# A long convolution by a two-factor Fourier transform, followed by a soft mixture of experts: the transform's length as 111 x 197 instead of 127 x 181

## The chip, the cores and the metric

One NeuronCore of a Trainium2 chip runs the whole program in one launch. Its engines are named as in the profile: PE is the matrix engine (PEld its loading of the stationary operand), DVE the vector engine, ACT the scalar engine, POOL the general engine, SP the engine whose queue issues nearly all DMAs here. The metric is the device time of one execution in microseconds (us).

## The reference

Everything is fp32. `x` and `v` are (4, 11456, 128); the filter is made by a small network from `pos_emb` (11456, 64). The convolution is causal and as long as the sequence, and its result goes through a mixture of 8 experts with 32 slots.

```python
B, S, D = x.shape
h_mlp = np.maximum(pos_emb @ w1, 0.0) @ w2
h_filt = h_mlp * np.exp(-0.01 * np.arange(S))[:, None]
u = x * v
y = irfft(rfft(u, n=2 * S, axis=1) * rfft(h_filt, n=2 * S, axis=0), n=2 * S, axis=1)[:, :S]
x = (x * y).reshape(B * S, D)
logits = x @ phi                                  # 45824 tokens x 32 slots
d = softmax(logits, over tokens); slot_input = d.T @ x
slot_out[e] = relu(slot_input[e] @ w1[e]) @ w2[e]  # 8 experts, 1024 hidden
out = softmax(logits, over slots) @ slot_out
```

## The kernel before

The transform has length L = N1 * N2 = 127 * 181, just over 2 * 11456. A position is written as 127 * j + r, with residues r from -63 to 63. Because both factors are odd and the data are real, only J = 91 = (181 + 1) / 2 frequencies of the long factor are kept and only R = 64 residues, each with its mirror image, so that one row of 2R = 128 holds r and -r. The 128 channels are worked on in G = 8 groups of 16; with 4 batches a group has C = 64 columns.

For a group there are four steps, each of which is a family of small fp32 matmuls. An fp32 matmul leaves two records in the trace, each with its own weight load, so that a count of 2048 records is 1024 matmuls.

- **p1** (function `first`, line 121): the sums and differences of x * v (tile `sd`, line 216; the product itself is made by POOL, line 213) are the stationary operand, JP = 96 rows of tokens by 128 residues; the cosine and sine table `tab1x` of 2J = 182 columns moves. 64 matmuls a group. ACT copies each result into `T` in three instructions for two channels (lines 125, 126 and 130), of 364, 182 and 182 elements a partition.
- **p2** (line 231): for each of the 91 frequencies one matmul, with the 127-column table `W[:, k, :]` stationary and 128 columns of `T` moving. DVE multiplies the result by the filter's spectrum `Hs` (line 236, two instructions for four frequencies), POOL combines the products and writes them back to `T` (lines 242 and 243).
- **p3** (line 249): 128 matmuls a group, 91 columns of `T` stationary, 2R = 128 columns of `tab3` moving; ACT copies one half (`ec`, line 253), DVE adds and subtracts into `E` (line 255).
- **p4** (line 279): two matmuls for each residue, 91 columns of `tab4` stationary, 128 columns of `E` moving, over JP = 96 rows of `E`, of which the last five are zeros that a DMA from `in_zero` put there once (line 342). DVE multiplies by `x` (line 285), and `p4_out` stores two blocks of 90 rows to the DRAM scratch `scr` (lines 293 and 297), plus one row left over in some cases (line 307). Residues go in blocks `rb` of eight, so there are eight of these.

The loop at line 313 shifts the steps by one group: its pass g first runs p1 of group g mixed with p3 of group g - 1 (16 units, each 8 matmuls of p3 and 4 of p1; called **stage A** below), then p4 of group g - 1 mixed with p2 of group g (**stage B**; the count `upto` at line 353 spreads the 23 blocks of p2 over the first 14 of 16 half blocks of p4). In pass 0 p1 runs alone, and p2 of group 0 is mixed with the making of the filter's spectra, which go to DRAM as `hs` (line 167) and come back as `Hs` in each stage A (line 320). Before that the filter itself goes through its network (`hid_step`, 16 steps of four residues), the first transform (`first` with `tab1h`, 32 calls) and the second (`filter_second`). In the last pass p3 and p4 of group 7 run alone while the experts' weights load. The mixture of experts follows in 24 blocks of at most 15 * 128 tokens.

What a reader needs of the order: engines take their instructions in order, and so does the SP queue; a framework orders what is not held by `inorder` by its own estimate of durations. The pool `ld` has five buffers for all tiles of x, v and xi, `st` has three for `sd` and `xo`, and the PSUM pools `psa` (p1, p2) and `psb` (p3, p4) four each. A load waits at the head of the SP queue until its buffer is free, and what is behind it waits too.

## Time and profile before

| | us |
|---|---|
| median of 3 runs (1159.65 to 1163.18) | 1161.48 |
| the profiled execution, its own time | 1160.11 |
| its span, first to last instruction | 1158.3 |
| PE busy (share of the span) | 1085.9 (94%) |
| PE weight loads busy | 1022.3 (88%) |
| DVE busy | 922.8 (80%) |
| ACT busy | 590.4 (51%) |
| POOL busy | 578.3 (50%) |
| mean granted PE clock, share of full | 0.962 |

The table is one average over stages that are limited by different things. The profile can be cut into stages by the line of the matmuls that run: the filter to 127 us, pass 0's p2 to 179, then seven pairs of stages A and B of some 50 us each to 892, the lone p3 and p4 of group 7 to 955, and the mixture of experts to the end. A busy PE is not a PE at its peak, since matmuls are pipelined and the duration of one record (0.25 to 0.33 us) is more than the distance between two; what one costs is read from the distance between starts.

### The profile page before, as it was taken

To read this page: it belongs to the slowest core of one execution; us is meant where nothing else is said; L and a number is where in the kernel's file an instruction comes from. 1 tells how busy PE (TensorE), PEld (TensorE's weight loads), DVE (VectorE), ACT (ScalarE), POOL (GpSimd) and SP (SyncE) were. 2 spreads that over 40 slices of the span, in tenths; PEclk is the share of its full clock that TensorE was granted. 3 is DMA by queue.
4 is the path that set the end of the run, shared out by engine and by line. 5 is a ranking of instruction groups with operands and counts; after the bars stand their busy time and mean duration, and the time that the engine had idled before them with its cause. 6 is when DMAs were issued, how large, how long until landed. Compare 5 with 4: busy or idle time off the path is not lost.

```text
span 1158.3 us, 25829 instructions
## 1 busy us (share of the span) xinstructions
PE 1085.9 (94%) x9237; PEld 1022.3 (88%) x9237; DVE 922.8 (80%) x1837; ACT 590.4 (51%) x1488; POOL 578.3 (50%) x712
## 2 busy tenths in 40 slices
PE   6999996999999999999999999999999989997997
PEld 6888895999999999999999999999999986655675
DVE  6346884978888897888879778887978848998797
ACT  0878873930770392086049118504910308876597
POOL 6102484437427544743754565275455004777774
PEclk9668997999999999999999999999999999999999
DMA  9522367523734562473355247236625668775388
GB/s 232 186 69 76 137 233 172 164 85 121 214 89 123 156 187 83 120 215 92 104 173 176 79 140 199 86 106 173 175 77 167 214 200 263 213 216 139 124 354 337
DMA packets 120993, 187.22 MB, mean 162 GB/s; under 512 B 14518, under 2 KB 67664, under 8 KB 120856
## 3 DMA queue, kind: packets, MB, share of 16 engines
q1 hardware_dynamic: 120538, 185.15, 52.3%
q8 instruction: 75, 1.23, 0.5%
q0 software_dynamic: 80, 0.30, 0.2%
q14 instruction: 52, 0.43, 0.1%
...
## 4 chain that ended last, share of the span: by engine, by line
PE 59%; DVE 17%; issue 7%; DMA 6%; ACT 6%; POOL 3%; SPq 1%; DVEq 0%; POOLq 0%; ACTq 0%
PE p L279 14%; PE p L231 12%; PE p L249 12%; PE p L121 11%; DVE E L255 6%; DMA v<-in_vf_dram 3%; PE fl L163 3%; ACT T L125 2%; PE f L136 2%; DVE sd L216 2%; PE ct L713 2%; DVE xreg L425 2%; PE pt L482 2%; ACT T L126 2%; DMA scr<-xo 1%
## 5 line engine op out<-in xcount | busy, mean ns | idle before, releaser
L253 ACT ACTIVATE ec<-p 91x256 f32<-91x256 f32 x256 | 90.2, 377 | 400.8 <-issue 344.9
L255 DVE TENSOR_TENSOR E<-p,ec 91x256 f32<-91x256 f32 x512 | 251.4, 606 | 34.1 <-ACT ec L253 33.6
L279 PE MATMUL p<-E,tab 96*91 96x128 f32 (+1 forms) x2048 | 243.9, 274 | 6.9 <-DVE E L255 6.9
L249 PE MATMUL p<-tab,T 127*91 127x128 f32 x2048 | 245.6, 275 | 2.4 <-POOL T L242 2.4
L242 POOL TENSOR_TENSOR T<-m,m 127x256 f32<-127x256 f32 (+1 forms) x184 | 137.6, 748 | 216.2 <-DVE m L236 195.3
L249 PEld LDWEIGHTS p<-tab,T 127*91 127x91 f32 x2048 | 237.4, 164 | 3.2 <-POOL T L242 2.6
L279 PEld LDWEIGHTS p<-E,tab 96*91 96x91 f32 x2048 | 231.1, 160 | 9.3 <-DVE E L255 6.5
L213 POOL TENSOR_TENSOR x<-x,v 96x512 f32<-96x512 f32 x112 | 145.4, 1299 | 149.9 <-DMA v<-in_vf_dram 113.9
L236 DVE TENSOR_TENSOR m<-p,T 127x512 f32<-127x512 f32 (+1 forms) x322 | 199.8, 679 | 22.6 <-issue 15.4
L121 PE MATMUL p<-tab1x,sd 96*128 96x182 f32 x1024 | 186.5, 326 | 23.6 <-DVE sd L216 22.5
L121 PEld LDWEIGHTS p<-tab1x,sd 96*128 96x128 f32 x1024 | 161.0, 194 | 30.1 <-DVE sd L216 15.3
L231 PE MATMUL p<-T,W 128*127 128x128 f32 x1456 | 185.4, 276 | 1.7 <-DVE T L128 1.7
L125 ACT ACTIVATE T<-p 64x364 f32<-64x364 f32 x288 | 154.2, 535 | 54.7 <-PE p L121 48.9
L231 PEld LDWEIGHTS p<-T,W 128*127 128x127 f32 x1456 | 175.2, 188 | 1.9 <-DVE T L128 1.9
L216 DVE TENSOR_TENSOR sd<-x 96x256 f32<-96x256 f32 x256 | 118.8, 503 | 35.5 <-POOL x L213 27.1
L285 DVE TENSOR_TENSOR xo<-p,xi 91x256 f32<-91x256 f32 (+1 forms) x256 | 95.9, 413 | 61.7 <-PE p L279 43.9
L243 POOL TENSOR_TENSOR T<-m,m 127x256 f32<-127x256 f32 (+1 forms) x184 | 137.5, 747 | 0.0
L126 ACT ACTIVATE T<-p 64x182 f32<-64x182 f32 x288 | 100.5, 349 | 3.4
L130 ACT ACTIVATE T<-p 64x182 f32<-64x182 f32 x224 | 70.4, 315 | 0.0
L530 POOL TENSOR_TENSOR E<-lt,mx 128x480 f32<-128x480 f32 (+1 forms) x24 | 24.6, 1024 | 75.1 <-DMA xreg<-scr 72.9
L483 ACT ACTIVATE E<-pt 128x512 f32<-128x512 f32 x96 | 49.1, 569 | 23.5 <-DVE xreg L425 19.2
L717 ACT ACTIVATE cs<-ct 96x512 fp32r<-96x512 f32 x96 | 53.3, 566 | 10.3 <-PE ct L713 6.9
(103 smaller groups left out, 1218.1 us busy)
## 6 DMA issues: line engine op xcount, KB each, us to landing
x<-in_xf_dram SPq DMA_DIRECT2D x128, 192.0 KB
xi<-in_xi_dram SPq DMA_DIRECT2D x128, 182.0 KB
...
v<-in_vf_dram SPq DMA_DIRECT2D x112, 192.0 KB
...
```

Source lines behind the costliest of these rows:

```text
L121: nc.tensor.matmul(ps[:, i].rearrange("p s k -> p (s k)"), lhsT=src(i), rhs=tab, start=True, stop=True)
L125: nc.scalar.activation(to[0:R], pq[0:R], AF.Copy)
L126: nc.scalar.activation(to[R:128, 0], pq[R:128, 1], AF.Copy)
L213: inorder(eng.tensor_tensor(out=xt, in0=xt, in1=vt, op=ALU.mult))
L216: add = nc.vector.tensor_tensor(out=sd[:, :, h : h + R], in0=xt[:, :, 0:R], in1=xt[:, :, R:], op=op)
L231: nc.tensor.matmul(ps[:, i].rearrange("p b c -> p (b c)"), lhsT=W[:, k0 + i, :], rhs=Tf[:, :, k0 + i, :], start=True, stop=True)
L236: nc.vector.tensor_mul(m[:, :n].rearrange("p k s c i -> p k (s c i)").rearrange("p k (b c) -> p k b c", c=CG), ps[:, :n], h[:, :, CG * s : ...
L242: nc.gpsimd.tensor_tensor(out=Ty[:, 0], in0=ms[0][:, :n, 0], in1=ms[1][:, :n, 1], op=ALU.subtract)
L243: nc.gpsimd.tensor_tensor(out=Ty[:, 1], in0=ms[1][:, :n, 0], in1=ms[0][:, :n, 1], op=ALU.add)
L249: nc.tensor.matmul(ps[:, i, 2 * s : 2 * s + 2, :].rearrange("p q r -> p (q r)"), lhsT=T[0:N1, s, c // CG, c % CG // 2, :, i], rhs=tab3[:, ...
L255: add = nc.vector.tensor_tensor(out=E[:J, :, 2 * s : 2 * s + 2, c : c + 2].rearrange("p r q c -> p c q r"), in0=ps[:, :, 0:2, :], in1=ec, ...
L279: nc.tensor.matmul(ps[:, i, :n], lhsT=tab4[:, s, o : o + J], rhs=E[:JP, r, s : s + 2 * n - 1 : 2, :], start=(s == 0), stop=(s == 1))
```

## The change

The length becomes 111 * 197 = 21867, less than 2 * 11456: what wraps round onto kept outputs comes from the filter's positions from 21867 - 11455 = 10412 on, where its window exp(-0.01 n) has died out. With it J goes from 91 to 99, R from 64 to 56. The folded tiles keep a row of 128 (`RP` = 64: 56 residues and eight zeros), so p1's stationary operand keeps its 128 columns; its rows are now JT = 105 tokens, loaded as JP = 112. Blocks of eight residues are seven, not eight.

| step, a group | before | after |
|---|---|---|
| p1 | 64 matmuls, 182 columns move | 64, 198 columns |
| p2 | 91 matmuls, 127 columns stationary, 128 move | 99, 111 stationary, 128 move |
| p3 | 128 matmuls, 91 stationary, 128 move | 128, 99 stationary, 112 move |
| p4 | 128 matmuls, 91 stationary, 128 move | 112, 105 stationary, 128 move |
| blocks of p2 (four frequencies) | 23 | 25, over the first 12 of 14 half blocks of p4 |
| x and v loads | 32 of 192 KB | 32 of 224 KB |
| `Hs` loads | 7 of 208 KB | 9 of 176 KB |
| xi loads | 16 of 182 KB | 14 of 224 KB |
| stores to `scr` | 2 of 90 rows a block | 4 a block: 96, 7, 96 and 7 rows |

The contraction of p4 takes the 99 rows of `E` that are written, so the zeros are not needed and both DMAs from `in_zero` go; the padding of `hid` is a POOL memset. The network of the filter runs 14 steps, its second transform 99 matmuls instead of 91. In the mixture of experts two small tiles move to another place, and the third block's load, in halves before, is issued whole after the seventh block of p4.

```diff
-N1, N2 = 127, 181
+N1, N2 = 111, 197
-J = 91
-JP = 96
-R = 64
+J = 99
+JT = 105
+JP = 112
+R = 56
+RP = 64
+FO = 64
...
-    nc.gpsimd.dma_start(out=moe.E[J:JP, : 2 * R * R], in_=zero[:, : 2 * R * R])
+    nc.gpsimd.memset(hid[:, :, R:RP], 0.0)
...
     def p1_load(g, u):
-        xt = ld.tile([JP, 4, 2 * R], F32, tag="ld", name=f"x_{g}_{u}")
+        xt = ld.tile([JP, 4, 2 * RP], F32, tag="ld", name=f"x_{g}_{u}")
...
-            first(lambda i: sd[:, h + i, :], tab1x, T[:, :, u // 4, 2 * (u % 4) + h // 2], g == 0)
+            first(lambda i: sd[:JT, h + i, :], tab1x, T[:, :, u // 4, 2 * (u % 4) + h // 2], g == 0)
...
-                nc.tensor.matmul(ps[:, i, :n], lhsT=tab4[:, s, o : o + J],
-                                 rhs=E[:JP, r, s : s + 2 * n - 1 : 2, :],
+                nc.tensor.matmul(ps[:, i, :n], lhsT=tab4[:, s, o : o + JT],
+                                 rhs=E[:J, r, s : s + 2 * n - 1 : 2, :],
...
     def p4_out(g, rb, xo):
...
+            for a, z in ((0, 96), (96, FULL)):
+                n = (z - a) * B * (8 - r0)
+                src = xo[s][2 * s + a : 2 * s + z]
...
-            nc.sync.dma_start(out=moe.E[J:JP], in_=zero)
...
-                upto = min(nk, (nk * (2 * t + h + 1)) // 14)
+                upto = min(nk, (nk * (2 * t + h + 1)) // 12)
...
-        if t >= 2:
+        if 2 <= t < 6:
             self.load(t // 2 - 1, G // 2 * (t % 2), G // 2 * (t % 2 + 1))
+        if t == 6:
+            self.load(2)
```

Besides the sizes, the order moves at three places. First, on PE at the start of stage A of group 2 (`p_1_...` from `tab` and `T` is p3 of group 1, `p_96` and on from `tab1x` and `sd` are the units of p1). Before:

```order
L121 MATMUL p_96_2797<-tab1x,sd_0_2760 128x182 x2
L121 MATMUL p_97_2803<-tab1x,sd_0_2760 128x182 x2
L249 MATMUL p_1_4_2817<-tab_79,T 91x128 x4
L249 MATMUL p_1_6_2826<-tab_79,T 91x128 x4
L249 MATMUL p_1_8_2855<-tab_79,T 91x128 x4
L249 MATMUL p_1_10_2864<-tab_79,T 91x128 x4
L249 MATMUL p_1_12_2893<-tab_79,T 91x128
L121 MATMUL p_98_2835<-tab1x,sd_1_2768 128x182 x2
L121 MATMUL p_99_2841<-tab1x,sd_1_2768 128x182 x2
L249 MATMUL p_1_12_2893<-tab_79,T 91x128 x3
L121 MATMUL p_100_2873<-tab1x,sd_2_2776 128x182 x2
```

Now:

```order
L126 MATMUL p_96_2854<-tab1x,sd_0_2817 128x198 x2
L126 MATMUL p_97_2860<-tab1x,sd_0_2817 128x198 x2
L254 MATMUL p_1_6_2883<-tab_79,T 99x112 x4
L254 MATMUL p_1_8_2912<-tab_79,T 99x112 x4
L254 MATMUL p_1_10_2921<-tab_79,T 99x112 x4
L254 MATMUL p_1_12_2950<-tab_79,T 99x112 x4
L254 MATMUL p_1_14_2959<-tab_79,T 99x112 x4
L254 MATMUL p_1_16_2989<-tab_79,T 99x112 x4
L126 MATMUL p_98_2892<-tab1x,sd_1_2825 128x198 x2
L126 MATMUL p_99_2898<-tab1x,sd_1_2825 128x198 x2
L254 MATMUL p_1_18_2998<-tab_79,T 99x112 x2
L126 MATMUL p_100_2930<-tab1x,sd_2_2833 128x198 x2
```

More of p3 stands ahead of the second unit of p1 than before (36 matmuls of p3 from the stage's start instead of 25), and units two to four follow close behind it.

Second, on SP at the end of stage B of the same pass, where the stores of group 1's last block (`xo_2_7`, now `xo_2_6`: the first number is the loop's pass) and the loads of the next stage A meet. Before:

```order
L293 DMA scr<-xo_2_7_3839 90x512
L297 DMA scr<-xo_2_7_3840 90x512
L307 DMA scr<-xo_2_7_3840 1x512
L211 DMA v_1_3876<-in_vf_dram 96x512
L201 DMA x_2_3882<-in_xf_dram 96x512
```

Now:

```order
L308 DMA scr<-xo_2_6_3901 96x512
L308 DMA scr<-xo_2_6_3901 7x512
L308 DMA scr<-xo_2_6_3902 96x512
L308 DMA scr<-xo_2_6_3902 7x512
L316 DMA scr<-xo_2_6_3902 1x512
L216 DMA v_1_3940<-in_vf_dram 112x512
L206 DMA x_2_3946<-in_xf_dram 112x512
```

The load of v for the second unit now stands behind five stores, not three.

Third, on SP at the start of stage A of group 1. Before:

```order
L167 DMA hs<-E 128x8x96
L211 DMA v_1_1654<-in_vf_dram 96x512
L201 DMA x_2_1660<-in_xf_dram 96x512
L211 DMA v_2_1662<-in_vf_dram 96x512
L342 DMA E<-in_zero_dram 5x16384
L201 DMA x_3_1698<-in_xf_dram 96x512
```

Now:

```order
L172 DMA hs<-E 128x8x96
L216 DMA v_1_1704<-in_vf_dram 112x512
L206 DMA x_2_1710<-in_xf_dram 112x512
L216 DMA v_2_1712<-in_vf_dram 112x512
L206 DMA x_3_1748<-in_xf_dram 112x512
```

The DMA of five rows of 64 KB of zeros, which stood among the loads of x and v, is gone.

## Rows read from the trace of the kernel before

**Rows 1.** The page's first part: busy us, share of the span, instructions.

```profile
PE 1085.9 (94%) x9237; PEld 1022.3 (88%) x9237; DVE 922.8 (80%) x1837; ACT 590.4 (51%) x1488; POOL 578.3 (50%) x712
```

**Rows 2.** Stages: us; busy (records): PE, PEld, DVE, ACT, POOL; clock; DMA.

```profile
0.00:29.60 29.60, 18.27 (x128) 17.83 (x129) 19.07 (x31) 1.28 (x1) 20.12 (x28) 0.93 0.91 235
29.60:73.20 43.60, 42.90 (x139) 37.45 (x139) 19.20 (x40) 39.99 (x64) 6.22 (x5) 0.58 0.39 136
...
126.70:179.10 52.40, 50.00 (x425) 49.81 (x425) 46.78 (x66) 34.29 (x63) 39.70 (x46) 1.00 0.71 238
179.10:240.20 61.10, 51.99 (x384) 50.85 (x384) 44.66 (x96) 43.17 (x126) 21.05 (x17) 0.89 0.58 141
...
289.10:340.30 51.20, 48.56 (x386) 47.79 (x384) 43.04 (x98) 43.01 (x125) 20.85 (x17) 1.00 0.57 168
340.30:389.20 48.90, 48.85 (x438) 48.81 (x439) 40.26 (x77) 1.03 (x3) 31.99 (x46) 1.00 0.36 108
891.80:922.30 30.50, 28.16 (x258) 27.94 (x256) 29.56 (x66) 12.14 (x32) 0.07 (x1) 1.00 0.69 220
922.30:955.30 33.00, 29.71 (x256) 29.52 (x257) 12.90 (x34) 0.52 (x1) 0.00 (x0) 0.92 0.70 213
955.30:1158.30 203.00, 180.04 (x1950) 131.75 (x1950) 175.97 (x319) 153.94 (x340) 134.08 (x193) 0.96 0.70 235
```

**Rows 3.** Timeline of PE in stage A: start us, us, what, records.

```profile
309.81 1.91 PE L249 MATMUL p<-tab,T 127*91 127x128 f32 x16
311.56 1.40 PE L121 MATMUL p<-tab1x,sd 96*128 96x182 f32 x8
312.79 1.91 PE L249 MATMUL p<-tab,T 127*91 127x128 f32 x16
```

**Rows 4.** Timeline of PE in stage B.

```profile
349.32 1.91 PE L279 MATMUL p<-E,tab 96*91 96x128 f32 x16
351.06 1.99 PE L231 MATMUL p<-T,W 128*127 128x128 f32 x16
352.90 0.82 PE L279 MATMUL p<-E,tab 96*91 96x128 f32 x6
```

**Rows 5.** Timeline of ACT, one late unit of stage A.

```profile
336.25 0.51 ACT L125 ACTIVATE T<-p 64x364 f32<-64x364 f32 x1
336.77 0.34 ACT L126 ACTIVATE T<-p 64x182 f32<-64x182 f32 x1
...
338.41 0.65 ACT L253 ACTIVATE ec<-p 91x256 f32<-91x256 f32 x2
339.24 0.50 ACT L125 ACTIVATE T<-p 64x364 f32<-64x364 f32 x1 [0.18 <-PE p L121]
```

**Rows 6.** Timeline at a stage A's start: SP's stores and load, PE's wait.

```profile
289.75 0.33 SPq L293 DMA_DIRECT2D scr<-xo  x1
...
290.89 0.32 SPq L211 DMA_DIRECT2D v<-in_vf_dram  x1
...
298.39 1.50 PE L121 MATMUL p<-tab1x,sd 96*128 96x182 f32 x8 [0.93 <-DVE sd L216]
```

**Rows 7.** Timeline of DVE, the middle of stage A: when sd is made.

```profile
315.29 0.76 DVE L216 TENSOR_TENSOR sd<-x 96x256 f32<-96x256 f32 x2
...
317.75 0.75 DVE L216 TENSOR_TENSOR sd<-x 96x256 f32<-96x256 f32 x2
```

**Rows 8.** Busy in 342 to 384 (stage B): all engines, DVE's L236 alone.

```profile
342.00:384.00 42.00, 42.00 (x379) 42.00 (x378) 35.90 (x68) 0.00 (x0) 27.56 (x40) 1.00 0.36 107
...
342.00:384.00 42.00, 26.11 (x42) 1.00 0.36 107
```

**Rows 9.** Timelines in stage A of group 1: the zeros' DMA on SP, POOL.

```profile
181.35 0.26 SPq L342 DMA_DIRECT2D E<-in_zero_dram  x1
...
195.17 2.48 POOL L213 TENSOR_TENSOR x<-x,v 96x512 f32<-96x512 f32 x2 [9.58 <-DMA v<-in_vf_dram]
```

**Rows 10.** Timeline of DVE in the lone p4 of group 7.

```profile
943.03 1.41 DVE L285 TENSOR_TENSOR xo<-p,xi 91x256 f32<-91x256 f32 x4 [2.19 <-DMA scr<-xo]
```

More of the change, by code (lines that the diff above doesn't have):

```diff
@@ L27 @@
 CH = C + CG
-ORG = 5778
+ORG = 5827
 TOK = B * S
@@ L31 @@
 NSLOT = 32
-ORDER = [1, 2, 3, 4, 5, 6, 7, 0]
-SQ = 2 * 90 * B * 8 // 128
-LEFT = 38
+ORDER = [1, 2, 3, 4, 5, 6, 0]
+FULL = 103
+SQ = 45
+LEFT = 33
 NEXP = 8
@@ L187, in conv_part @@
     Td = Th.rearrange("p k (s f) -> p s k f", s=2)
-    for f in range(0, R, 2):
-        if f < 26:
-            ks = slice(7 * (f // 2), 7 * (f // 2) + 7)
+    for f in range(0, FO, 2):
+        if f < 22:
+            ks = slice(9 * (f // 2), 9 * (f // 2) + 9)
             inorder(nc.sync.dma_start(out=W[:, ks, :], in_=wt[:, ks, :]))
@@ L287, in p4 @@
                 ps[:, i:, s, :].rearrange("p r (b c) -> p r b c", b=B),
-                xs[s][:, :, rs, :].rearrange("p b r c -> p r b c"))
+                xs[s][:JT, :, rs, :].rearrange("p b r c -> p r b c"))
     def p4_out(g, rb, xo):
-        t0 = 128 * SQ * ORDER.index(rb)
-        n = 90 * B * 8
-        nc.sync.dma_start(out=scr[g, t0 : t0 + n, :].rearrange("(p b r) c -> p (b r c)", b=B, r=8),
-                          in_=xo[0][0:90].rearrange("p b r c -> p (b r c)"))
-        t0 += n
-        if rb:
-            nc.sync.dma_start(out=scr[g, t0 : t0 + n, :].rearrange("(p b r) c -> p (b r c)", b=B, r=8),
-                              in_=xo[1][1:J].rearrange("p b r c -> p (b r c)"))
-        else:
-            n = 90 * B * 7
-            nc.sync.dma_start(out=scr[g, t0 : t0 + n, :].rearrange("(p b r) c -> p b (r c)", b=B, r=7),
-                              in_=xo[1][1:J, :, 1:, :].rearrange("p b r c -> p b (r c)"))
+        t0 = sum(2 * FULL * B * 8 - (0 if i else FULL * B) for i in ORDER[: ORDER.index(rb)])
+        for s in range(2):
+            r0 = 1 if s and not rb else 0
+            for a, z in ((0, 96), (96, FULL)):
+                n = (z - a) * B * (8 - r0)
+                src = xo[s][2 * s + a : 2 * s + z]
+                if r0:
+                    nc.sync.dma_start(
+                        out=scr[g, t0 : t0 + n, :].rearrange("(p b r) c -> p b (r c)", b=B, r=8 - r0),
+                        in_=src[:, :, r0:, :].rearrange("p b r c -> p b (r c)"))
+                else:
+                    nc.sync.dma_start(
+                        out=scr[g, t0 : t0 + n, :].rearrange("(p b r) c -> p (b r c)", b=B, r=8),
+                        in_=src.rearrange("p b r c -> p (b r c)"))
+                t0 += n
         lo = max(0, LEFT - 8 * rb)
@@ L356, in conv_part @@
                     done += 1
-                if h == 0 and t < 7:
+                if h == 0 and t + 1 < len(rbs):
                     nxt = p4_load(g - 1, rbs[t + 1])
@@ L462, in _moe @@
            for i in range(2)]
-    acc = mp.tile([128, 128], F32, tag="acc", name="acc")
+    acc, sop = (mo.xreg[:, (XB + OB) * 2 * FF + 128 * i :][:, :128] for i in range(2))
     neg = mp.tile([128, NBL + 1], F32, tag="neg", name="neg")
@@ L740, in _constants @@
     f = np.float32
[L741 removed]
+    tj = np.arange(-(JT // 2), JT // 2 + 1)
     k2 = np.arange(J)
@@ L819, in _rows @@
         r = slice(8 * rb, 8 * rb + 8)
-        one += [p[:90, None, r] + off, m[1:, None, max(1, 8 * rb) : 8 * rb + 8] + off]
-    one += [m[:1, None, max(LEFT, 8 * rb) : 8 * rb + 8] + off for rb in range(LEFT // 8, 8)]
+        one += [p[:FULL, None, r] + off, m[2:, None, max(1, 8 * rb) : 8 * rb + 8] + off]
+    one += [m[1:2, None, max(LEFT, 8 * rb) : 8 * rb + 8] + off for rb in range(LEFT // 8, R // 8)]
     one = np.concatenate([a.reshape(-1) for a in one])
```

109 lines of the change are left out of this document (52 added, 57 removed).

## The prediction

> **What bounds the kernel now.** I read the page's first part, then the busy time by stage, then timelines inside a stage. The first part says that PE works 94% of the span, with DVE at 80% [rows 1]. By stage the picture is sharper. A stage B takes 48.90 us, of which PE is busy 48.85, with DVE at 40.26 and ACT at nothing; a stage A takes 51.20, with PE at 48.56, DVE at 43.04 and ACT at 43.01 (the windows from 289.10 and 340.30 [rows 2]). So seven pairs A and B, 700 of the 1160 us, are PE's, and what the change does to them is first a matter of how far apart matmul records start.
>
> That distance comes from the timeline. In A, 16 records of p3 start at 309.81 and p1 at 311.56: 1.75 / 16 = 0.1094 us each; then 8 records of p1 to 312.79: 0.154 each [rows 3]. In B, 16 records of p4 take 351.06 - 349.32 = 1.74, 0.109 each, and 16 of p2 take 1.84, 0.115 each [rows 4]. p1, p3 and p4 go by the columns that move: 128 cost 0.1094, 182 cost 0.154, so a column is worth (0.154 - 0.1094) / 54 = 0.83 ns. The number of contracted rows does not show: p3 has 127 and p4 has 96, at the same 0.109. p2 moves 128 columns like p3 and p4 yet takes 5 to 6 ns more; it differs by a stationary operand of 127 columns instead of 91, and by reading `T` in strides.
>
> These distances explain the stages. A: 256 records of p3 and 128 of p1 are 28.0 + 19.7 = 47.7; the other 3.5 lie at the start, where PE waits for the first units' `sd` (0.93 before the second unit [rows 6]), and at the change to B. B: 256 x 0.109 + 182 x 0.115 = 48.8 of 48.9.
>
> **The change part by part.** New distances: p3 with 112 columns 0.1094 - 16 x 0.00083 = 0.0962; p1 with 198 columns 0.167; p4 0.109 as before. For p2 the bounds are 0.109 (wide weights were the cause; 111 columns are between the 91 that cost nothing extra and 127) and 0.115 (the strides are the cause). I take 0.109, because all other rows are explained by columns alone.
>
> *Stage B*, seven times: p4 falls from 256 records to 224 (-3.5 us), p2 goes from 182 x 0.115 = 20.9 to 198 x 0.109 = 21.6. PE's sum is 24.4 + 21.6 = 46.0, which is 2.8 less. DVE is next: in 42 us it is busy 35.90, of which 26.11 are 42 instructions of line 236 (0.622 each) and the other 9.79 are 26 of line 285 (0.377) [rows 8]. A half block of p4 now carries 25 / 12 = 2.08 blocks of p2, each with two products: 4.17 x 0.622 + 2 x 0.377 = 3.35 us of DVE against 16 x 0.109 + 16.7 x 0.109 = 3.56 of PE. DVE is at 94% there, against 85% now; I give 0.3 us a stage for that and take **-2.5 x 7 = -17.5** (bounds: -20, and -11 if p2 stays at 0.115).
>
> *Stage A*, seven times: PE's sum is 256 x 0.0962 + 128 x 0.167 = 46.0, or 2.875 us for each of 16 units against 2.98. That is 1.7 less, but two things eat it. ACT: a late unit's work runs from 336.25 to the end of its second `ec` at 339.24 - 0.18 = 339.06, which is 2.81 us [rows 5]. Line 125 takes 0.51 for 364 elements and line 126 0.34 for 182 [rows 5], about 1 ns an element; the copies of a unit grow by 2 x (32 + 16 + 16) = 128 elements, +0.13, and its two `ec` shrink by 32 each, -0.06. So ACT needs 2.88: level with PE, with no slack for either, and I take 2.91 a unit, 16 x 0.07 = 1.1 gained. The start: v of the second unit was issued at 290.89, behind three stores of which the first was issued at 289.75, so 0.38 an issue [rows 6]. Five stores are there now, so this load, the product, `sd` and with them PE come 0.76 later. Having 36 instead of 25 matmuls of p3 ahead of that unit hides nothing in the end, since units two to four now come close behind it and each needs its own load. Sum -0.3, **-2 in seven** (bounds: -12 with PE's full gain and no delay, +8 with a unit of 2.98).
>
> *Group 1's stage A* takes 61.10, group 2's 51.20 [rows 2]. The zeros are issued at 181.35; a load of v queued behind them lands so late that POOL has idled 9.58 us when it goes on at 195.17 [rows 9], and PE with it. In no other stage A is there such a DMA, or such a wait. With the zeros gone the wait goes: **-8** (bounds -9.6, and -5 if the loads, also queued among the last writes of `hs`, are late by themselves).
>
> *The start.* The network: 14 steps instead of 16, wider by 8/91. The stage ends by 29.60 with 16 steps [rows 2], so two steps are worth at most 3.7; some of it is the loads: **-2** (bounds -3.7, 0). The filter's first transform is ACT's: 64 instructions in 39.99 us [rows 2], 1.25 a call for 546 elements; 594 now, at most +9% or 3.6, at 1 ns an element +1.5: **+2.5** (PE is as busy there, at a granted clock of 0.58, and its bound is the same +9%). Its second: 16 more records at about p2's distance, **+1.8**. p1 of group 0: 128 records x 13 ns, **+1.7**. Pass 0's p2 with the filter's last step: 8 more frequencies are 16 + 24 records, at 0.115 +4.6; records with 111 stationary columns may be faster, but DVE is at 46.78 of 52.40 there [rows 2], so **+2** (bounds +0.6, +4.6). The memset on POOL in place of a DMA lies before the first product of `hid` and costs nothing while the loads are awaited; its bound is under one product, 1 us.
>
> *The last pass.* The lone p3 is DVE's: 66 instructions, 29.56 of 30.50 us [rows 2], 0.448 each; 32 elements less out of 256 are 0.03 (at 1 ns) to 0.056 (in proportion), 64 times: **-2** (bounds -2, -3.6). The lone p4 takes 33.0 for 256 records (27.9 by distance), because DVE waits for stores to free `xo`, 2.19 at the longest [rows 10]. One block in eight goes (-4.1), but each of its stores is now two, so the queue holds two more issues of 0.38 a block, 5.3 in all if each delays DVE; I take 3 of them. **-1** (bounds -4, +1).
>
> *The mixture of experts* is 203 us [rows 2] of unchanged work; the third block's load comes whole, in the same place behind the last block of p4: **0** (bounds -1, +1.5).
>
> Sum: -17.5 - 2 - 8 - 2 + 2.5 + 1.8 + 1.7 + 2 - 2 - 1 = -24.5. Against the profiled execution's 1160.1 that is 1135.6; the median lies 1.4 above this execution, so I forecast 1137.
>
> **The rivals.**
>
> *PE keeps its whole gain.* ACT and DVE keep pace, the p3 run covers the later load, the lone p4 follows PE. Stage A gives -12, B -20, p2 of group 0 +0.6, the lone p4 -3: 16 us more than above, 1121. For it: late units of A and all of B are PE's to within 1% today. Against it: ACT at 2.88 of 2.875.
>
> *p2 stays at 0.115.* The distance is that of a matmul that reads `T` in pairs of elements, whatever the weights are. B then gains 48.8 - (24.4 + 198 x 0.115) = 1.6 instead of 2.5, and group 0 loses 1.2: 7.5 us less in all, 1145. The Trainium skill speaks for this one (TensorE: Matmul & The Clock Gate, "LDWEIGHTS (loading the stationary operand)": a load takes columns / 1.2 ns, 106 ns for 127 columns by my estimate, which would hide under 109). The rows do not settle it; that 91 columns cost nothing extra fits both.
>
> *Stage A's units stay at 2.98 or above*, since ACT and PE, both without slack, wait for each other in turn. Then A costs +0.8 a stage instead of -0.3: +8 us, 1145; with the p2 case as well 1153.
>
> *Slower: the loads set stage A.* The loop is: a buffer of `ld` comes free, x and v load, POOL multiplies, DVE makes `sd` and frees it. While `Hs` loads, `sd` comes every 317.75 - 315.29 = 2.46 us [rows 7], faster than PE needs it. x and v grow by a sixth, which makes 2.87 if the loop is all loading: just level with PE. To lose the whole gain a unit has to take 24 / 7 / 16 = 0.21 more than my 2.91, so 3.12 is the point from which it decides, a loop 27% longer; at 3.2 (+30%) it costs 16 x 0.29 x 7 = 32 us: 1169. Against it: DMA is at 57% over an A [rows 2].
>
> **How the numbers follow.** A measurement of this kernel tells about 0.3% (3.5 us) from no change. Forecast 1137 (1128 to 1142): 0.50. PE's whole gain, around 1121: 0.20. One of the two smaller gains, 1142 to 1155: 0.22. Between 1158 and 1165 (both smaller gains, and little from the zeros): 0.03. Slower by the loads: 0.05. So faster 0.92, same 0.03, slower 0.05. The range 1119 to 1152 leaves out the slower and the unchanged case and the end of the smaller gains (0.12 together) and the far end of PE's whole gain (0.08).
>
> **What would show it.** In the new trace, distances of 96, 167 and 109 ns for p3, p1 and p4, and p2 at 109 or 115; stages B of 46.4, stages A (group 2 on) of 51, with ACT's idle time in late units near nothing; group 1's stage A no longer 10 us above the others; the lone p3 at 28.5; the part before 127 us longer by 4. Wrong would be: a stage A longer than 52 with POOL or DVE waiting for loads (the slower rival), or DVE busy all through B with PE waiting on `psa`.

## The result, and the profile after

| | us |
|---|---|
| before, median of 14 runs (1157.38 to 1166.17) | 1162.45 |
| after, median of 14 runs (1144.95 to 1159.05) | 1148.45 |
| ratio, with its 95% interval | 0.9895 (0.9872 to 0.9918) |
| the same two kernels a second time, ratio | 0.9881 (0.9851 to 0.9912) |

The change gains 12 to 14 us, where 24.5 were forecast: the time lies within the range, but the gain is about half the size. The first part of the page of the changed kernel, to be held against [rows 1]:

```profile
PE 1076.8 (93%) x9133; PEld 1005.2 (87%) x9133; DVE 895.9 (77%) x1835; ACT 603.8 (52%) x1496; POOL 603.1 (52%) x742
```

PE lost 9 us of busy time. By stage (us; busy (records) of PE, PEld, DVE, ACT, POOL; granted clock; DMA), read as in [rows 2]; the window from 386.90 is group 3's stage A, those from 338.10 and 643.30 are stages B:

```profile
0.00:24.80 24.80, 15.26 (x113) 14.21 (x113) 17.38 (x27) 1.28 (x1) 19.35 (x26) 1.00 0.87 270
127.10:184.70 57.60, 55.21 (x472) 55.00 (x472) 47.11 (x72) 38.02 (x70) 45.62 (x50) 1.00 0.70 234
184.70:237.30 52.60, 50.20 (x385) 49.40 (x385) 42.75 (x96) 44.32 (x126) 21.20 (x17) 0.94 0.63 186
338.10:386.90 48.80, 48.80 (x423) 48.74 (x423) 40.82 (x77) 0.90 (x3) 34.34 (x50) 0.97 0.37 109
386.90:439.80 52.90, 48.43 (x387) 46.64 (x385) 40.47 (x98) 43.65 (x126) 20.94 (x17) 1.00 0.64 188
643.30:690.40 47.10, 47.10 (x422) 47.10 (x422) 40.80 (x77) 0.95 (x3) 34.20 (x50) 1.00 0.38 113
```

Two things are seen at once: a stage A is longer than before at full clock, 52.90 for group 3 against 51.00 for the same group before, though PE has less to do in it; and a stage B comes in two lengths, 47.1 at full clock and 48.8 where the clock is at 0.97.

This profiled execution is the longest of the fourteen. The same kernel was profiled again among the experiments (a_again, 1145.85 us, close to the median), and the table of terms is made from both. Each entry is the stage's length less that of the kernel before.

| part | forecast | first profile | second profile |
|---|---|---|---|
| start, to group 0's p2 (126.7 before) | +4.0 | +0.4 | -1.1 |
| pass 0's p2 and the filter's last step (52.4) | +2 | +5.2 | +5.2 |
| stage A of group 1 (61.1) | -8.3 | -8.5 | -10.3 |
| stages A of groups 2 to 7 (307.9) | -1.8 | +11.2 | +8.2 |
| seven stages B (343.8) | -17.5 | -5.6 | -10.4 |
| lone p3 (30.5) | -2 | -3.0 | -3.0 |
| lone p4 (33.0) | -1 | -3.1 | -4.5 |
| mixture of experts (202.9) | 0 | +2.1 | +1.4 |
| sum | -24.6 | -1.3 | -14.5 |

So the miss has two main places: stages A of groups 2 to 7, 10 us off the forecast in the second profile, and stages B, 7 us off. Pass 0 is 3 us off the same way. Against these, the start, group 1's stage A and the lone p3 and p4 gained 11.6 us more than was forecast; that the time still lies in the range is luck in that part. One experiment (before_no_zeros) needs a word on its time: in its profiled execution TensorE ran at half clock for 58 us from the lone p4 on, and three more of its six executions were as long at as low a mean clock, so its ratio is that of the other two, and of its profile only rows ahead of that place are used.

What goes on in a stage A is read from its start. Rows of the timeline of the changed kernel (start us, us, engine and line, what, instructions, idle time before and its releaser), group 3's stage, which begins at 386.9:

```profile
387.51 1.47 SPq L308 DMA_DIRECT2D scr<-xo  x4
389.32 0.32 SPq L216 DMA_DIRECT2D v<-in_vf_dram  x1
389.78 2.10 DVE L260 TENSOR_TENSOR E<-p,ec 99x224 f32<-99x224 f32 x5
391.36 5.16 PE L254 MATMUL p<-tab,T 111*99 111x112 f32 x48
392.06 1.28 POOL L218 TENSOR_TENSOR x<-x,v 112x512 f32<-112x512 f32 x1 [3.46 <-DMA v<-in_vf_dram]
393.64 2.95 DVE L260 TENSOR_TENSOR E<-p,ec 99x224 f32<-99x224 f32 x7 [1.76 <-ACT ec L258]
396.43 1.56 DVE L221 TENSOR_TENSOR sd<-x 112x256 f32<-112x256 f32 x2
398.02 0.31 SPq L206 DMA_DIRECT2D x<-in_xf_dram  x1
398.05 1.61 PE L126 MATMUL p<-tab1x,sd 105*128 105x198 f32 x8 [1.53 <-DVE sd L221]
401.78 1.27 POOL L218 TENSOR_TENSOR x<-x,v 112x512 f32<-112x512 f32 x1 [4.40 <-DMA v<-in_vf_dram]
```

Unit 1's v is issued at 389.32 behind the last block's five stores (four in the row, the left-over row's at 389.02), lands, and POOL's product of it is done at 392.06 + 1.28 = 393.34. DVE is idle just then, but in its order twelve adds of p3 stand between unit 0's sums and unit 1's, and seven of them are still to come; the sums start at 396.43, 3.1 us after the product. PE waits 1.53 for them. The sums also free unit 1's x buffer: SP issues the next x at 398.02, 0.03 us after they end, and POOL waits 4.40 us for what comes behind it. One late instruction on DVE so delays two units.

The kernel before has eight adds there (the same stage, which begins at 389.2):

```profile
391.23 1.94 DVE L255 TENSOR_TENSOR E<-p,ec 91x256 f32<-91x256 f32 x4
394.91 1.96 DVE L255 TENSOR_TENSOR E<-p,ec 91x256 f32<-91x256 f32 x4 [1.75 <-ACT ec L253]
396.72 0.94 DVE L216 TENSOR_TENSOR sd<-x 96x256 f32<-96x256 f32 x2
```

Its sums come 1.0 us after their product, and PE waits for them too: 0.9 to 1.6 us in groups 2 to 7, against 1.5 to 1.8 in the first profile of the changed kernel and 0.7 to 2.2 in the second. So the wait is not new; it grew, and others came with it.

### The profile page after: what moved, and what is told of

Same layout as the page of the kernel before. It is cut to its first block, busy times and chain, and to the rows that moved or that the text cites. A ratio compares the mean times of both kernels' runs of the same rounds, so it can differ in the third digit from the quotient of the medians.

```text
span 1156.9 us, 25846 instructions
## 1 busy us (share of the span) xinstructions
PE 1076.8 (93%) x9133; PEld 1005.2 (87%) x9133; DVE 895.9 (77%) x1835; ACT 603.8 (52%) x1496; POOL 603.1 (52%) x742
## 4 chain that ended last, share of the span: by engine, by line
PE 40%; issue 21%; DVE 16%; DMA 10%; ACT 9%; POOL 4%; SPq 1%; POOLq 0%; DVEq 0%; ACTq 0%
PE p L284 8%; PE p L236 8%; DMA v<-in_vf_dram 8%; PE p L254 7%; PE p L126 6%; DVE E L260 5%; ACT T L130 4%; PE fl L168 3%; POOL x L218 3%; ACT T L131 3%; PE f L141 2%; PE ct L722 2%; DVE sd L221 2%; DVE xreg L433 2%; DVE xreg L738 1%
## 5 line engine op out<-in xcount | busy, mean ns | idle before, releaser
L260 DVE TENSOR_TENSOR E<-p,ec 99x224 f32<-99x224 f32 x512 | 221.9, 550 | 43.3 <-ACT ec L258 42.7
L247 POOL TENSOR_TENSOR T<-m,m 111x256 f32<-111x256 f32 (+1 forms) x200 | 146.2, 731 | 187.5 <-DVE m L241 135.8
L241 DVE TENSOR_TENSOR m<-p,T 111x512 f32<-111x512 f32 (+1 forms) x350 | 216.0, 678 | 24.5 <-issue 16.3
L254 PE MATMUL p<-tab,T 111*99 111x112 f32 x2048 | 222.0, 262 | 8.7 <-DVE E L260 4.5
L254 PEld LDWEIGHTS p<-tab,T 111*99 111x99 f32 x2048 | 214.5, 171 | 14.5 <-issue 7.1
L284 PE MATMUL p<-E,tab 99*105 99x128 f32 (+1 forms) x1792 | 215.7, 276 | 11.5 <-DVE E L260 11.5
L126 PE MATMUL p<-tab1x,sd 105*128 105x198 f32 x1024 | 200.8, 342 | 18.7 <-DVE sd L221 16.4
L284 PEld LDWEIGHTS p<-E,tab 99*105 99x105 f32 x1792 | 205.4, 173 | 13.8 <-DVE E L260 11.4
L236 PE MATMUL p<-T,W 128*111 128x128 f32 x1584 | 202.2, 280 | 1.4 <-DVE T L133 1.4
L236 PEld LDWEIGHTS p<-T,W 128*111 128x111 f32 x1584 | 192.2, 178 | 1.6 <-DVE T L133 1.6
L248 POOL TENSOR_TENSOR T<-m,m 111x256 f32<-111x256 f32 (+1 forms) x200 | 156.7, 783 | 0.0
L540 POOL TENSOR_TENSOR E<-lt,mx 128x480 f32<-128x480 f32 (+1 forms) x24 | 24.6, 1026 | 70.0 <-ACT et L522 67.0
```

The source lines that it names most:

```text
L126: nc.tensor.matmul(ps[:, i].rearrange("p s k -> p (s k)"), lhsT=src(i), rhs=tab, start=True, stop=True)
L236: nc.tensor.matmul(ps[:, i].rearrange("p b c -> p (b c)"), lhsT=W[:, k0 + i, :], rhs=Tf[:, :, k0 + i, :], start=True, stop=True)
L241: nc.vector.tensor_mul(m[:, :n].rearrange("p k s c i -> p k (s c i)").rearrange("p k (b c) -> p k b c", c=CG), ps[:, :n], h[:, :, CG * s : ...
L247: nc.gpsimd.tensor_tensor(out=Ty[:, 0], in0=ms[0][:, :n, 0], in1=ms[1][:, :n, 1], op=ALU.subtract)
L248: nc.gpsimd.tensor_tensor(out=Ty[:, 1], in0=ms[1][:, :n, 0], in1=ms[0][:, :n, 1], op=ALU.add)
L254: nc.tensor.matmul(ps[:, i, 2 * s : 2 * s + 2, :].rearrange("p q r -> p (q r)"), lhsT=T[0:N1, s, c // CG, c % CG // 2, :, i], rhs=tab3[:, ...
```

## Experiments

The theories: (1) the order on DVE and PE at the start of a stage A, which the framework chose anew after the change (12 adds between the sums of unit 0 and of unit 1, where the kernel before has 8); (2) the two more stores a block, which stand ahead of v; (3) ACT's longer copies; (4), formed after the first four runs, the five buffers of the loads. For p2's distance: the width of the stationary operand, the rows, or the strided reading of `T`.

**a_again**: the changed kernel unchanged.

> The changed kernel itself, unchanged, for a second profile and a time on the chip of this group of runs. The one profile so far was the longest of its executions (span 1156.9 us, mean granted clock 0.962) and has six stretches of 3.4 us at half clock at the start of a stage B or in a stage A. If those stretches belong to the program, they stand in this profile too, at the same places (338.6, 441.0, 543.4 us and so on), and the span is within 3 us of 1156.9. If they belong to that execution, most are missing here, stage B lasts 47.3 us wherever they are missing, and the span is 1143 to 1150 us. Both expect a ratio to the kernel before of 0.987 to 0.992 and stages A of 52.5 to 54 us.

1147.50 us. Of the stages from group 2 on, the stretches at half clock do not stand at the same places: of the six stages B behind a gap of 1.4 to 1.7 us, five began at half clock in the first profile, two in this one (from 432.0 and 534.4), and the others last 47.2. So the stretches belong to the execution, and the length of the wait ahead of them does not decide alone whether one comes. Stages A from group 2 on are 51.2 to 54.4 long, so what lengthens them is in the program.

**stores7_act**: the short stores issued by ACT.

```diff
+                q = nc.scalar if a else nc.sync
...
-                    nc.sync.dma_start(
+                    q.dma_start(
```

> The stores of the last seven token rows (one in two of those in stage B) are issued from ScalarE's queue and not from SyncE's. Theory 2 (the two more stores and the larger loads delay the first products of stage A): unit 0's and 1's v land 0.5 to 1 us sooner, stage A is 0.5 to 1 us shorter, and the time falls by 4 to 7 us against the changed kernel. Theories 1 and 3: unit 1's product was done at 291.64 us, 2.3 us before VectorE came to it, so the time stays within 2 us; issued on ScalarE, which has work without a pause in the stage, each store costs it some issue time, so that it may also rise by up to 3 us.

1146.40 us, ratio 0.9873 (0.9840 to 0.9905): the same as the changed kernel. It is not a clean test, since the framework set another order with it: unit 1's sums come early here, and the wait went to unit 2. Timeline of group 3's stage:

```profile
391.12 2.53 POOL L218 TENSOR_TENSOR x<-x,v 112x512 f32<-112x512 f32 x2 [3.65 <-DMA v<-in_vf_dram]
392.42 1.84 DVE L221 TENSOR_TENSOR sd<-x 112x256 f32<-112x256 f32 x2 [1.74 <-POOL x L218]
394.32 1.61 PE L126 MATMUL p<-tab1x,sd 105*128 105x198 f32 x8 [2.67 <-DVE sd L221]
```

Here the product itself is late, and the sums follow it at once: a product can be late in its own right. Unit 1's v is issued 1.7 us into the stage instead of 2.4, as theory 2 expected, but the time did not fall by the 4 to 7 us that it gave. Since the order changed with it, this run does not tell what the two stores cost by themselves.

**sums_first**: the sums of unit u + 1 directly behind the adds of unit u, throughout.

```diff
+    def p1_sums(g, u, xt):
...
-            if g == 0:
-                inorder(add)
+            inorder(add)
...
+            sds = {0: p1_sums(*xts.pop(0))}
...
+                if u + 1 < NU:
+                    sds[u + 1] = p1_sums(*xts.pop(u + 1))
```

> Only VectorE's order in stage A is set by hand: the sums of unit u + 1 stand directly behind the inverse transform's adds of unit u, so that they no longer wait behind seven adds at the start of a stage. Theory 1 (order): stage A is 2 us longer than forecast because unit 1's sums come 2.1 us after unit 1's product is there; then TensorE's wait ahead of unit 1's first transform falls from 1.77 to below 0.6 us, each of the stages A from the second on is 1 to 2 us shorter, and the time falls by 6 to 14 us against the changed kernel. Theory 2 (loads): the product itself comes late, since the loads stand behind two more stores; then the wait stays within 0.5 us of 1.77 and the time within 3 us. Theory 3 (ScalarE's copies alone): the wait at the start falls, but stage A still ends when ScalarE has made 16 times 2.8 us of copies, and the time falls by less than 4 us.

1155.50 us, ratio 0.9959 (0.9930 to 0.9988): 8 us slower than the changed kernel, a miss for all three. The gap at the stage's end did go (0.2 to 0.3 us ahead of stages B from group 2 on), but inside the stage PE now waits for the sums of several units. Timeline of group 6's stage:

```profile
707.77 1.58 PE L126 MATMUL p<-tab1x,sd 105*128 105x198 f32 x8 [1.50 <-DVE sd L224]
712.35 1.28 POOL L218 TENSOR_TENSOR x<-x,v 112x512 f32<-112x512 f32 x1 [2.70 <-DMA v<-in_vf_dram]
```

With every unit's sums behind all adds of the unit before, each x buffer is freed late and POOL waits for v far into the stage. The edit moved 16 units to cure one: the place of the sums matters, and one can also err to the other side.

**copy_split**: half of ACT's third copies to DVE.

```diff
-            first(lambda i: sd[:JT, h + i, :], tab1x, T[:, :, u // 4, 2 * (u % 4) + h // 2], g == 0)
+            first(lambda i: sd[:JT, h + i, :], tab1x, T[:, :, u // 4, 2 * (u % 4) + h // 2], g == 0 or h == 0)
```

> Half of the third copies of T (354 ns each, two in a unit) go from ScalarE to VectorE in stage A. ScalarE's unit falls from 2.77 to about 2.4 us, VectorE's rises by about 0.35 us and stays below 2.4. Theory 3 (ScalarE's copies hold stage A and leave it late): the gap ahead of the output transform at the end of A falls from 1.5 to about 0.5 us, the stretches at half clock behind it go, stage A is 1 to 2 us and stage B up to 1.6 us shorter, and the time falls by 8 to 20 us against the changed kernel. Theory 1 (VectorE's order at the start): the 1.77 us wait for unit 1's sums stays, the end's gap falls, and the time falls by 4 to 10 us. A unit stays at 2.89 us under either, since TensorE's own work fills it. VectorE's longer queue could also push the sums back: then the time rises by up to 5 us.

1165.56 us, ratio 1.0052 (1.0031 to 1.0074), 18 us slower than the changed kernel. One of its stages A (columns as above):

```profile
492.10:546.80 54.70, 49.04 (x386) 46.55 (x384) 47.18 (x113) 40.87 (x110) 20.95 (x17) 1.00 0.65 182
```

ACT has 2.8 us less in a stage than in the row above (40.87 against 43.65), DVE 6.7 more, and PE waits 8.3 us in all for DVE to free p3's results, against 4.5 in the first profile. The gap ahead of stage B stayed, at 1.65 us. Relief for ACT that DVE pays for makes the stage longer. That does not yet clear ACT's copies as the cause of the long stage; sd1_early below, which leaves them as they are, does.

**ld_7 and before_ld_7**: seven buffers in `ld`, in either kernel.

```diff
-    ld = ctx.enter_context(tc.tile_pool(name="ld", bufs=5))
+    ld = ctx.enter_context(tc.tile_pool(name="ld", bufs=7))
```

> The pool that holds the loaded x, v and the factors of the output (ld) gets seven buffers in place of five, in the changed kernel. In the traces so far v of unit 1 is issued only behind the last output products of stage B, which free its buffer, and the x of unit 3 only behind unit 1's sums; GpSimd waits 3.5 and 4.4 us for v at the start of a stage A, and TensorE 1.8 us or more for unit 1's sums in all of the changed kernel, sums_first and stores7_act. Theory 4 (buffers of the loads): then both waits of GpSimd fall below 1 us, TensorE's waits in the first 20 us of a stage A from 3 us to below 1, stage A at full clock from 52 to 53 us to 49.5 to 50.5, and the time by 10 to 18 us against the changed kernel (1130 to 1138). Theory 1 (VectorE's order alone): with the buffers the scheduler also puts unit 1's sums four adds behind unit 0's and not twelve, so the same gain, but GpSimd's waits for v stay above 2 us. Theory 3 (ScalarE's copies): stage A stays above 52 us whatever the loads do, and the gap ahead of stage B at 1.4 us.

> The same seven buffers in the kernel before. If the late loads at the start of a stage A are a loss that both kernels have, it gains too: TensorE's waits of 1.2 to 2.5 us a stage go, stage A falls from 51.2 to about 49.5 us, the time by 6 to 12 us. If the loss came with the change (the larger loads and the two more stores), the kernel before gains less than 3 us.

ld_7 takes 1130.62 us, ratio 0.9748 (0.9723 to 0.9773), 15 to 17 less than the changed kernel (by the ratios and by the medians); before_ld_7 takes 1153.65, ratio 0.9940 (0.9921 to 0.9960), 7 less than the kernel before. A stage A of ld_7, and the start of group 6's at 671.8:

```profile
280.90:331.60 50.70, 47.52 (x386) 46.48 (x384) 43.77 (x98) 43.29 (x126) 21.58 (x17) 1.00 0.76 196
```

```profile
672.26 2.50 POOL L218 TENSOR_TENSOR x<-x,v 112x512 f32<-112x512 f32 x2
675.44 1.61 PE L126 MATMUL p<-tab1x,sd 105*128 105x198 f32 x8 [1.29 <-DVE sd L221]
```

POOL makes the first two products back to back, and at the start PE waits 1.29 us for unit 0's sums and not at all for unit 1's. Its stages A from group 2 on are 49.7 to 50.7 long, just under the 50.9 of the forecast. With the buffers the framework also puts unit 1's sums earlier (4 adds behind unit 0's), so this run alone does not tell theory 1 from 4; POOL still waits 2.43 us for v ahead of its fourth product, which was theory 1's sign. In the kernel before, six stages A fall by 2.5 us together (305.4 against 307.9), in the changed kernel by 14 (302.3 against 316.1 in its second profile): nearly all of what the buffers cure came with the change. The rest of before_ld_7's 7 us lies elsewhere, 1.7 of it in a stretch at half clock that its stages B don't have and 3.5 behind the lone p3; I did not follow it.

**sd1_early**: order alone, five buffers. Eight adds of p3 (c = 6 to 12) are held behind unit 1's sums on DVE, and the matmuls of c = 14 behind its p1 on PE.

```diff
+        if u == 1:
+            behind[g] = add.ins
...
+        with tc.issue_after(behind[g + 1, 0]) if 0 < g < G - 1 and c == 14 else ExitStack():
...
+        with tc.issue_after(behind[g + 1]) if 0 < g < G - 1 and c in (6, 8, 10, 12) else ExitStack():
```

> Order alone, with the five buffers of the changed kernel: in the stages A from the second on unit 1's sums stand behind 5 of the inverse transform's adds and not 12, and unit 1's first transform behind 16 of its matmuls and not 24. Theory 1 (order): unit 1's sums are made as soon as its product is there, TensorE's wait for them falls from 1.8 to 2.0 us to below 0.6, the buffer that they free lets the x of unit 3 go 3 us earlier, stage A falls to 50 to 51 us and the time by 8 to 12 us against the changed kernel (near 1137). Theory 4 (buffers of the loads): the product itself is bound by v, so the wait only moves to units 1 to 3, stage A stays at 52 us or more and the time within 4 us, as it did in sums_first.

1133.31 us, ratio 0.9777 (0.9747 to 0.9806), 12 to 14 less than the changed kernel. Group 6's stage, which begins at 676.8, for comparison with the rows of 386.9 above:

```profile
683.29 0.76 DVE L224 TENSOR_TENSOR sd<-x 112x256 f32<-112x256 f32 x2 [1.50 <-POOL x L221]
684.08 0.98 SPq L209 DMA_DIRECT2D x<-in_xf_dram  x1
684.33 1.52 PE L126 MATMUL p<-tab1x,sd 105*128 105x198 f32 x8
716.85 1.29 POOL L221 TENSOR_TENSOR x<-x,v 112x512 f32<-112x512 f32 x1 [2.06 <-DMA v<-in_vf_dram]
```

From the stage's start unit 1's sums stand at 6.5 us instead of 9.5, the x behind them is issued at 7.3 instead of 11.1, PE does not wait for unit 1, and POOL's longest wait for v behind the first falls from 4.4 us to 2.1. Loads, stores, buffers and copies are those of the changed kernel. Its six stages A from group 2 on take 304.7 us, against 316.1 in a_again and 307.9 before. Theory 1 is shown for the changed kernel: most of what ld_7 gains comes with the order alone. Two of the six stages stay at 52.0 and 52.8; in the longer one POOL still waits 4.4 us for unit 1's v, as theory 4 had it. The edit moves DVE's order and PE's together and does not tell them apart, and it was not made in the kernel before.

**end_split, ld_7_end, ld_7_vec0**: what is left. The first two move four of ACT's copies at the end of a stage to DVE, in the changed kernel and in ld_7; the third moves unit 0's product in ld_7.

```diff
-            first(lambda i: sd[:JT, h + i, :], tab1x, T[:, :, u // 4, 2 * (u % 4) + h // 2], g == 0)
+            first(lambda i: sd[:JT, h + i, :], tab1x, T[:, :, u // 4, 2 * (u % 4) + h // 2],
+                  g == 0 or u >= NU - 4 and h == 0)
```

```diff
-        eng = nc.vector if g == 0 and u % 3 == 2 else nc.gpsimd
+        eng = nc.vector if (u == 0 if g else u % 3 == 2) else nc.gpsimd
```

> The changed kernel, with four of the third copies of T (one each in the last four units of a stage A) on VectorE and not on ScalarE: ScalarE has 1.4 us less at the end of the stage. Theory 3 for the gap (ScalarE is late with the last ec, and the output transform waits for the adds behind it): the gap ahead of stage B falls from 1.4 to 1.7 us to 0.6 or less, no stage B starts at half clock any more, and the time falls by 5 to 10 us against the changed kernel. If VectorE itself is late there, the gap stays above 1.2 us and the time within 3 us, or rises.

> ld_7 with the four third copies on VectorE that end_split moves. In ld_7 the gap ahead of stage B is 0.5 to 1.5 us (mean 1.0) with no stretch at half clock behind it. Theory 3 for the gap: it falls to 0.6 in all, the time by 2 to 4 us against ld_7. If VectorE sets it: within 1.5 us or slower.

> ld_7, and the product of unit 0 on VectorE and not on GpSimd in the stages A from the second on. In ld_7 one wait is the same in all of them, 1.55 us of TensorE for unit 0's sums at 3.6 us from the stage's start. If it is GpSimd's, which makes the last parts of T until 0.4 us into the stage and only then the product (1.28 us), the wait falls below 0.5 us, stage A from 50.4 to about 49.3, and the time by 5 to 8 us against ld_7 (1123 to 1126). If v's landing sets it, the time stays within 2 us of ld_7.

end_split: 1146.50 us, ratio 0.9884 (0.9852 to 0.9915), no change; the gap ahead of stage B scatters between 0.44 and 1.70 us and one stage B still starts at half clock. ld_7_end: 1129.01 us, ratio 0.9722 (0.9693 to 0.9752), the fastest kernel here, 1.6 below ld_7, which the intervals do not tell apart. Its gaps ahead of the stages B of groups 2 to 7 are 0.31, 0.45, 1.05, 0.32, 0.95 and 0.54 against 1.45, 1.11, 1.46, 0.52, 1.15 and 0.74 in ld_7. The end of a stage A on the timeline, first in the changed kernel (group 3), then in ld_7_end (group 2):

```profile
436.83 1.52 PE L126 MATMUL p<-tab1x,sd 105*128 105x198 f32 x8
437.68 0.33 ACT L135 ACTIVATE T<-p 64x198 f32<-64x198 f32 x1
438.03 0.60 ACT L258 ACTIVATE ec<-p 99x224 f32<-99x224 f32 x2
438.42 1.69 DVE L260 TENSOR_TENSOR E<-p,ec 99x224 f32<-99x224 f32 x4 [1.01 <-ACT ec L258]
439.77 2.09 PE L284 MATMUL p<-E,tab 99*105 99x64 f32 x14 [1.42 <-DVE E L260]
```

```profile
327.54 1.52 PE L126 MATMUL p<-tab1x,sd 105*128 105x198 f32 x8
327.61 0.61 ACT L259 ACTIVATE ec<-p 99x224 f32<-99x224 f32 x2
328.00 1.70 DVE L261 TENSOR_TENSOR E<-p,ec 99x224 f32<-99x224 f32 x4 [0.67 <-ACT ec L259]
329.37 1.84 PE L285 MATMUL p<-E,tab 99*105 99x64 f32 x15 [0.31 <-DVE E L261]
```

In the changed kernel ACT comes to the last `ec` 1.2 us after PE has gone on to p1 (438.03 against 436.83), straight from another copy: it is behind. Here it comes 0.07 after. The relief takes the mean gap from 1.07 to 0.60 us, so ACT's backlog is part of the gap; two of the six gaps stay near 1. In sums_first the gap went without any relief for ACT, so the order has a part in it too.

ld_7_vec0: 1135.07 us, ratio 0.9781 (0.9753 to 0.9810), 4 slower than ld_7, a miss. Unit 0's wait went in five of the six stages (0.35 us is left in group 7's), but the order that came with it makes PE wait 1.1 to 3.2 us for unit 2 in every stage from group 2 on, as on the timeline of group 5's:

```profile
588.37 1.61 PE L126 MATMUL p<-tab1x,sd 105*128 105x198 f32 x8 [1.65 <-DVE sd L221]
```

**before_no_zeros**: one part of the change alone.

```diff
-    nc.gpsimd.dma_start(out=moe.E[J:JP, : 2 * R * R], in_=zero[:, : 2 * R * R])
...
-                nc.tensor.matmul(ps[:, i, :n], lhsT=tab4[:, s, o : o + J],
-                                 rhs=E[:JP, r, s : s + 2 * n - 1 : 2, :],
+                nc.tensor.matmul(ps[:, i, :n], lhsT=tab4[:J, s, o : o + J],
+                                 rhs=E[:J, r, s : s + 2 * n - 1 : 2, :],
...
-            nc.sync.dma_start(out=moe.E[J:JP], in_=zero)
```

> The kernel before, with the output transform and the first transform of the filter over the 91 rows that carry numbers and not over 96, and both loads of zeros left out: one part of the change alone. The prediction gave it 8 us: the first stage A (61.1 us, with one wait of 9.6 us for v behind the five packets of zeros) falls to 52 to 53 us, the other stages stay within 0.3 us, and the time falls by 7 to 9 us against the kernel before. If v was late for another reason, the stage stays above 58 us.

Ratio 0.9847 (0.9812 to 0.9881), from two executions. Two of its stages, the start and group 1's stage A, and PE's wait in that stage A of the kernel before:

```profile
0.00:25.00 25.00, 16.53 (x128) 15.50 (x128) 18.74 (x31) 1.28 (x1) 20.13 (x27) 0.97 0.92 284
176.00:227.00 51.00, 50.15 (x384) 49.40 (x385) 44.00 (x96) 42.98 (x126) 21.88 (x17) 0.97 0.53 163
```

```profile
198.41 0.94 PE L121 MATMUL p<-tab1x,sd 96*128 96x182 f32 x2 [8.56 <-DVE sd L216]
```

Group 1's stage A falls by 10.1 us, 2 more than was forecast: from 192.4 on the clock had been at half for 10.2 us, 6 of them in PE's long wait and 4.2 behind it (0.89 over the stage [rows 2], 0.97 now). And the first transform of the filter starts at 25.0 instead of 29.6. With the other load of zeros, at the very start, 4.6 us go that the forecast had not seen; 3.1 of them are left at group 0's p2. The other six stages A are 2.0 us longer together, not within 0.3 each as expected.

The ratio says more than these stages. It is as low as that of the whole change (0.9881, 0.9851 to 0.9912): as far as two executions tell, leaving out the zeros alone gives all that the change gave, and the new length, with the order that came with it, adds nothing that can be measured. Only with the order set (sd1_early, 0.9777) does the time fall below that of the zeros alone.

**p2_forms**: four forms of p2, by group.

```diff
+            z = 120 if g % 4 > 1 else 128
+            rhs = Tall[:z, 128 * (k0 + i) : 128 * (k0 + i) + 128] if g % 2 else Tf[:z, :, k0 + i, :]
```

> The changed kernel with four forms of the second transform's matmuls, by group: groups 0 and 4 as it is, 1 and 5 read T as 128 numbers in a row and not 99 apart, 2 and 6 use 120 rows and not 128, 3 and 7 both (the odd groups give other numbers). The records of this transform stand 114 ns apart in both kernels, with 127 or 111 columns of weights, against 109 for the output transform's with as many moving columns. If the strided reading of T sets it, groups 1, 3, 5 and 7 show 108 to 110 ns and the others 114. If the 128 rows do, groups 2, 3, 6 and 7 show 108 to 110. If neither, all show 113 to 115. A stage B has 198 such records, so 1 us hangs on it in each.

Its time (1371.6) says nothing, since the reading in a row takes in other numbers of `T`, which POOL is still writing, and waits for them. The distances do. Timeline of PE: group 5, in a row, 128 rows of `T`; then group 6, in strides, 120 rows:

```profile
751.97 0.91 PE L238 MATMUL p<-T,W 128*111 128x128 f32 x6 [0.29 <-POOL T L249]
752.72 2.35 PE L286 MATMUL p<-E,tab 99*105 99x128 f32 x20
755.20 1.34 PE L238 MATMUL p<-T,W 128*111 128x128 f32 x10
756.38 1.91 PE L286 MATMUL p<-E,tab 99*105 99x128 f32 x16
...
902.11 2.00 PE L238 MATMUL p<-T,W 120*111 120x128 f32 x16
903.95 1.91 PE L286 MATMUL p<-E,tab 99*105 99x128 f32 x16
```

In a row, 10 records take 1.18 us and 6 take 0.75, so four more cost 0.43 or 0.108 each. In strides 16 take 1.84, 0.115 each. Over all records not behind a wait and at full clock the median is 109 ns in the odd groups and 114 in the even, with 120 rows as with 128: the reading of `T` in pairs costs 5 ns a record.

## Why the prediction was right or wrong

*Right.* p3, p1 and p4 go by the columns that move. In the changed kernel 16 records of p3 take 1.53 us (0.096), 8 of p1 1.36 (0.170), 16 of p4 1.74 (0.109), forecast as 0.0962, 0.167 and 0.109:

```profile
309.73 1.70 PE L254 MATMUL p<-tab,T 111*99 111x112 f32 x16
311.26 1.52 PE L126 MATMUL p<-tab1x,sd 105*128 105x198 f32 x8
312.62 0.55 PE L254 MATMUL p<-tab,T 111*99 111x112 f32 x4
...
346.89 1.91 PE L284 MATMUL p<-E,tab 99*105 99x128 f32 x16
348.63 1.99 PE L236 MATMUL p<-T,W 128*111 128x128 f32 x16
350.47 1.91 PE L284 MATMUL p<-E,tab 99*105 99x128 f32 x16
```

The filter's first and second transforms together with group 0's p1 (+2.0 and +1.8 in the second profile, forecast +2.5 and +3.5), the lone p3 and the mixture of experts came within 2 us. Stage B is PE's at full clock, as forecast.

*Wrong: p2's distance.* The step of the prediction "I take 0.109, because all other rows are explained by columns alone" chose the wrong end. It is 1.84 / 16 = 0.115 in the rows just above, with 111 columns as with 127, and p2_forms shows the cause, the strides. The rival "p2 stays at 0.115" had it, with the right price: a stage B at full clock falls by 1.7 (48.9 to 47.2), forecast of the rival 1.6. The rule of the Trainium skill that the prediction names (TensorE: Matmul & The Clock Gate, "LDWEIGHTS (loading the stationary operand)") fits: the width of the weights does not show. A second page of the Trainium skill bears on the strides (Advanced Engine Details and Errata, "SBUF Cachelines"): full speed wants further accesses in the same line of 16 bytes, at least two a line. Here each line gets two, a pair of fp32, and the record is still 5 ns longer, so the measurement decides against that rule. The step costs 5.6 us of the 7 missing in stages B; the rest is half clock, in two of them against one before. In pass 0 the same step, with 30 more of the filter's last matmuls behind the first p2 (273 against 243; the forecast counted 24) at 0.12 us, makes 30 x 0.12 + 16 x 0.114 = 5.4 against the 5.2 measured, where 2 were taken and 4.6 stood as the bound.

*Wrong: stage A.* The step that failed is "Having 36 instead of 25 matmuls of p3 ahead of that unit hides nothing in the end". It treated the longer run of p3 as idle cover, at no cost. On DVE it is work that stands ahead of unit 1's sums, and those sums free the buffer that later loads wait for. The other half of that step, 0.76 us for two more stores ahead of v, is not what decides: with the short stores off the queue the time was the same, and with the stores left in place one edit of the order gained 12 to 14 us. The size of the unit was right: where the waits are gone a stage A takes 49.6 to 50.7 (four of sd1_early's six from group 2 on, all of ld_7's), forecast 50.9. By the distances, 256 records of p3 save 3.4 us and 128 of p1 cost 2.0, a gain of 1.4; the second profile's stages take 52.7 on average, 51.3 before, so 2.8 us a stage stand against it. Of these 0.8 are the gap ahead of stage B (1.5 on average against 0.7 before), 0.3 the longer wait for unit 1 and 0.3 a stretch at half clock; the rest I did not trace to single waits. The forecast saw that ACT has no slack, but priced it as a slower unit and not as a backlog that can come due at the stage's end. Its bound of +8 for seven stages does not follow from its own terms either: a unit of 2.98 leaves 7 x 0.76 = 5.3; the +8 is the distance from the -2 taken.

The two other rivals: "slower: the loads set stage A" has the right loop (buffer, load, product, sums), but it binds only the first units, and the point from which it decides was not reached. Its sign, a stage A longer than 52 with POOL waiting for loads, did come (52.90, with 4.40 us of waiting for v), by way of the order. "Stage A's units stay at 2.98" and the p2 rival each gave 1145, near the measured 1148, and both together 1153. For stage A the reason was wrong; the p2 rival had the right mechanism, but not the one that cost most, so that its time came near is partly luck.

*Sizes.* The zeros were worth 10 us in group 1's stage A and 4.6 at the start, forecast 8 and nothing. The first transform starts at 29.6 in both kernels with zeros and at 24.1 to 25.0 in every one without, the latest being before_no_zeros with all 16 steps; so the two steps that the network lost, forecast at -2, were worth 0.2 to 0.9. The lone p4 gave 3.1 to 4.5, forecast 1: 3 us for two more issues a block was too much.

*Open.* What decides whether a stretch at half clock follows the gap ahead of stage B. It costs 1.6 us in a stage B, and stretches stand six times in the longest execution's stages B and A from group 2 on and three times in the one near the median. None of ld_7's and ld_7_end's stages from group 2 to the lone p3 had one, though two of ld_7's gaps were 1.45 and 1.46. Open too is how much the same edit of the order would gain in the kernel before.
